# Query stage of a linear-attention and feed-forward kernel: the product with the key sums and the remainder of the tail weights on GpSimd, the tails stored in three transfers, the masked states made by PSUM bank

## The chip, the cores and the metric

The kernel runs on one core of one Trainium2 chip. The metric is the device time of one execution in microseconds (us). The unchanged kernel takes 1645.51 us, the median of three runs (1642.47 to 1647.66).

## The reference

Two networks are computed from independent inputs in float32. The first is a linear attention over 2048 rows of 576 columns with 32 heads of 18 columns: for queries and keys a learned 18x18 map per head and a double softmax (of the result and of its negative) give 36 features; the values are summed with the key features into a state per head, and the key features alone into key sums.

```
pq = einsum("bhsd,hdf->bhsf", q, w_phi); phi_q = concat(softmax(pq), softmax(-pq))    # the same for the keys
kv = einsum("bhsf,bhsd->bhfd", phi_k, v);  z = einsum("bhsf->bhf", phi_k)
num = einsum("bhqf,bhfd->bhqd", phi_q, kv)
den = einsum("bhqf,bhf->bhq", phi_q, z) + 1e-6
y = (num / den) @ wo
```

The second is a feed-forward network on rows of 576 columns with 4608 hidden columns: silu(x @ w_gate) * (x @ w_up), then @ w_down.

## The kernel before

Every float32 product on TensorE is made of parts: a value is split into a high part in TensorE's rounded format (a cast, mostly on ACT) and a remainder (a subtraction, mostly on DVE). A helper `split` does this, so many different instructions have its lines 58 and 59; `xw` issues products of the input with split weights, all under line 92.

The first 480 us hold the preparation, the key and value stage, and the **query stage**, from about 226 us. The key and value stage leaves the sums in three PSUM banks `kvp`, four, four and two blocks of up to 126 rows; one column more than the block is wide holds the key sums. At the boundary between the stages the key sums are copied out (`zc`), broadcast over 128 rows by matmuls with a 0/1 matrix (`ident`), and copied to `zb`; the states are multiplied with a mask that keeps the blocks of a head (`km`) and split into `KVH` and `KVL`.

The query stage takes 16 tiles of 128 rows, in pairs. For each tile `q_tile` does 28 matmuls with the folded query weights QH and QL into the one PSUM pair `p2`. This pair has no second buffer: the next tile's matmuls start when DVE's second subtraction `e<-p` has read the last of it. DVE and ACT make the softmax parts `e` (128x1152, both signs); `ez` is the product of `e` with `zb`, reduced over a head's columns to `y`; from it come the denominators, and `e` is scaled by them. `numer` then transposes `e` (`pt`), splits it (`ph`, `pl`), multiplies with the states (`po`) and splits the result (`oh`, `ol`); `project` multiplies with the split output weights `WOH` and `WOL`, and ACT copies the result (`so`) and stores it (`s_dram`). TensorE has other work to put between: gate and up products of five slices of the feed-forward network (`pe`), whose activation ACT and DVE finish (`h`) and whose weights ACT and DVE split (`wh`, `wl` from `raw`).

The stage also prepares eight **tails**, weight columns that the feed-forward network later reads back from device memory (`t_dram`). For each, SP loads 128x512 into the tile `tl` (two buffers), GpSimd forms three more blocks by four subtractions, ACT casts the 128x896 tile to `th` (one buffer), DVE subtracts `th` from `tl`, and GpSimd issues twelve stores of 32 rows: `th` twice and the remainder `tl` once, four each.

Within an engine instructions run in the order written. The order on each engine is set when the program is built: a scheduler places the instructions by dependence, by priority and by its own costs, and `tc.issue_after` bounds where the tails may go. A change of engine or of cost can thus move other instructions too. SP issues all loads of this stage and a share of the stores, ACT the stores of `so`.

Of the kernel before, what the change touches and what calls it, by code (L numbers as in the profile page):

```python
# [9 lines left out]
F32 = mybir.dt.float32  # L10
# [3 lines left out]
AX = mybir.AxisListType  # L14
PSUM = bass.MemoryType.PSUM

S, D, H, DH, F = 2048, 576, 32, 18, 4608
P = 128
# [7 lines left out]
GW = GH * DH  # L26
GROUPS = [(g * GW, min(GW, D - g * GW)) for g in range((D + GW - 1) // GW)]
NG = len(GROUPS)
# [9 lines left out]
def heads(ap):  # L38
    return ap.rearrange("p (h d) -> p h d", d=DH)


def spread(ap, n):
    return ap.unsqueeze(2).to_broadcast([P, n, DH])
# [3 lines left out]
def gated_hedgehog_kernel(ctx: ExitStack, tc, x, w_qk, w_v, w_phi, wo, w_gu, w_tail, w_down, ident_in, mask_in, out):  # L47
# [5 lines left out]
    nc = tc.nc  # L53
# [3 lines left out]
    def split(hi, lo, src):  # L57
        nc.scalar.copy(hi, src)  # L58
        nc.vector.tensor_sub(lo, src, hi)  # L59
# [15 lines left out]
    t_dram = dram.tile([TAILS, 4, 3, 32, 7, P], F32, name="t_dram")  # L75
# [3 lines left out]
    def block(t):  # L79
        return t // HT, (t % HT) // 4, slice((t % 4) * P, (t % 4 + 1) * P)  # L80

    def xw(ps, i, j, cols, wh, wl, stationary_x):
        pairs = []
        for k in range(2):
            b = XB[i][2 * j + k]
            for c in range(2):
                pairs += [(b[:, c, cols], w[:, k, c]) for w in (wh, wl)]
                pairs += [(b[:, 3 + c, cols], wh[:, k, c])]
            pairs += [(b[0:96, 2, cols], wh[0:96, k, 2])]
        for n, (a, b) in enumerate(pairs):  # L90
            l, r = (a, b) if stationary_x else (b, a)
            last = nc.tensor.matmul(ps, l, r, start=n == 0, stop=n == len(pairs) - 1)  # L92
        return last
# [32 lines left out]
    with ExitStack() as att:  # L126
        const = att.enter_context(tc.tile_pool(name="const", bufs=1))
        ident = const.tile([P, P], F32, name="ident")
# [3 lines left out]
        mask = const.tile([GW, GH, DH], F32, name="mask")  # L132
# [3 lines left out]
        with ExitStack() as wst:  # L136
# [4 lines left out]
            with ExitStack() as pst:  # L141
# [104 lines left out]
                for n in range(6):  # L246
                    k, c = divmod(n, 3)
                    src, vh = wv[n][:, 0:D], KVWH[:, k, c, D:2 * D]
# [18 lines left out]
            kps = kst.enter_context(tc.tile_pool(name="kps", bufs=1, space=PSUM, reuse_waits="tile"))  # L267
# [5 lines left out]
            def softmax_parts(ps, e):  # L273
                m = kk_pool.tile([P, 2, H], F32, name="m", bufs=1)
                p4 = ps[:, :, 0:HALF].rearrange("p a (h d) -> p a h d", d=DH)
                for s, op in enumerate((ALU.max, ALU.min)):
                    m3 = m[:, s].rearrange("p (a h) -> p a h", a=2)
                    nc.vector.tensor_reduce(m3, p4, axis=AX.X, op=op)
                    read.append(nc.vector.tensor_sub(e[:, s * D:(s + 1) * D].rearrange("p (a h d) -> p a h d", a=2, d=DH),
                                                     p4, m3.unsqueeze(3).to_broadcast([P, 2, H // 2, DH])))  # L280
                for s in range(2):
                    nc.scalar.activation(e[:, s * D:(s + 1) * D], e[:, s * D:(s + 1) * D], AF.Exp,
                                         scale=1.0 if s == 0 else -1.0)
                sm = kk_pool.tile([P, 2 * H], F32, name="sm")
                nc.vector.reduce_sum(sm, heads(e), axis=AX.X)
                nc.vector.reciprocal(sm, sm)
                return sm
# [137 lines left out]
            kvp = []  # L425
            pend = None
            order = [6, 7, 0, 1, 2, 3, 4, 5]
            for p in range(8):
# [29 lines left out]
                vx, vy, vw = (kps.tile([P, 512], F32, name=n) for n in ("vx", "vy", "vw"))  # L458
# [32 lines left out]
        with ExitStack():  # L491
            qc = att.enter_context(tc.tile_pool(name="qc", bufs=1, reuse_waits="tile"))
            KVH = qc.tile([GW, 2 * NG, GW], F32R, name="KVH")
            KVL = qc.tile([GW, 2 * NG, GW], F32R, name="KVL")
            zb = qc.tile([P, 2 * D], F32, name="zb")
            zc = qc.tile([GW, 2 * NG], F32, name="zc")
            for i in range(3):
                for j in range(4 if i < 2 else 2):
                    w = GROUPS[(4 * i + j) // 2][1]
                    nc.scalar.copy(zc[0:w, 4 * i + j:4 * i + j + 1], kvp[i][0:w, j, w:w + 1])  # L500
            for s in range(2):
                for a, m, name in ((0, 4, ("p2", "vw")[s]), (4, 1, ("vy", "vx")[s])):
                    o, w = GROUPS[a]
                    zp = kps.tile([P, 512], F32, name=name)
                    for g in range(a, a + m):
                        nc.tensor.matmul(zp[:, (g - a) * GW:(g - a) * GW + w],
                                         zc[0:w, 2 * g + s:2 * g + s + 1].to_broadcast([w, P]), ident[0:w, 0:w],
                                         start=True, stop=True)
                    nc.scalar.copy(zb[:, s * D + o:s * D + o + m * w], zp[:, 0:m * w])
            for i in range(2 * NG):  # L510
                o, w = GROUPS[i // 2]
                km = qc.tile([GW, GW], F32, name="km", bufs=2)
                nc.vector.tensor_mul(km[0:w, 0:w], kvp[i // 4][0:w, i % 4, 0:w],
                                     mask.rearrange("p h d -> p (h d)")[0:w, 0:w])
                split(KVH[0:w, i, 0:w], KVL[0:w, i, 0:w], km[0:w, 0:w])

        raw_x(order[7], 0, 1)
        raw_x(order[7], 2, 3)
# [4 lines left out]
        with ExitStack() as qst:  # L523
            qw = qst.enter_context(tc.tile_pool(name="qw", bufs=1, reuse_waits="tile"))
            qk = qst.enter_context(tc.tile_pool(name="qk", bufs=2, reuse_waits="tile"))
# [1 line left out]
            WOH = qw.tile([GW, NG, D], F32R, name="WOH")  # L527
            WOL = qw.tile([GW, NG, D], F32R, name="WOL")
            wrs = [qk.tile([P, 2, D], F32, name="oh", bufs=1), qk.tile([P, 2, D], F32, name="ol", bufs=1),
                   qk.tile([P, 2, D], F32, name="ez", bufs=1)]  # L530
            for g, (o, w) in enumerate(GROUPS):
                nc.sync.dma_start(wrs[g // 2][0:w, g % 2], wo[o:o + w, :])

# [8 lines left out]
            def tails(n):  # L542
                t = qk.tile([P, 7, P], F32, name="tl", bufs=2)
                hi = qk.tile([P, 7, P], F32R, name="th", bufs=1)
                nc.sync.dma_start(t[:, 0:4], w_tail[n])
                sub = nc.gpsimd.tensor_sub
                sub(t[:, 4], t[:, 2], t[:, 0])
                sub(t[:, 2], t[:, 3], t[:, 2])
                sub(t[:, 5], t[:, 3], t[:, 4])
                sub(t[:, 6], t[:, 1], t[:, 5])  # L550
                nc.scalar.copy(hi, t)
                nc.vector.tensor_sub(t, t, hi)
                for b, src in enumerate((hi.bitcast(F32), hi.bitcast(F32), t)):
                    for q in range(4):
                        nc.gpsimd.dma_start(t_dram[n, q, b], src[32 * q:32 * q + 32])

            last_e = []

            def q_tile(t):
                i0, j0, cols = block(t)  # L560
                pq = qps.tile([P, 2, 512], F32, name="p2")
                for i in range(2):
                    w = slice(i * HALF, (i + 1) * HALF)
                    xw(pq[:, i, 0:HALF], i0, j0, cols, QH[:, :, :, w], QL[:, :, :, w], True)
                e = qk.tile([P, 2 * D], F32, name="e", bufs=4)
                r = softmax_parts(pq, e)
                ez = qk.tile([P, 2 * D], F32, name="ez", bufs=1)
                nc.vector.tensor_mul(ez, e, zb)
                y = qk.tile([P, 2 * H], F32, name="y")
                nc.vector.reduce_sum(y, heads(ez), axis=AX.X)  # L570
                nc.vector.tensor_mul(y, y, r)
                den = qk.tile([P, H], F32, name="den")
                nc.vector.scalar_tensor_tensor(den, y[:, 0:H], DEN_EPS, y[:, H:], op0=ALU.add, op1=ALU.add)
                nc.vector.reciprocal(den, den)
                nc.vector.tensor_mul(r.rearrange("p (s h) -> p s h", s=2), r.rearrange("p (s h) -> p s h", s=2),
                                     den.unsqueeze(1).to_broadcast([P, 2, H]))
                last_e.append(nc.vector.tensor_mul(heads(e), heads(e), spread(r, 2 * H)))
                return e
# [55 lines left out]
            for n in range(TAILS):  # L634
                with tc.issue_after(last_e[3 * n // 2 + 2].ins):
                    tails(n)
# [82 lines left out]
    def stored(src, fill):  # L719
        h = h_tile()  # L720
        for r in range(2):
            nc.sync.dma_start(h[r], src[:, r * BT:(r + 1) * BT])
        for _ in range(2):
            fill()
        return h
# [280 lines left out]
    for i, n, f in units:  # L1006
# [3 lines left out]
        if f >= EARLY:  # L1010
            w = kept.pop() if i and kept else ready.pop(0)
# [4 lines left out]
        h = stored(h_dram[i, f], fill) if f < EARLY else gate_up(w, xo, fill, (i, f) == (0, EARLY))  # L1016
        if n % 2 == 0:
            g = {"f": (f, units[units.index((i, n, f)) + 1][2]), "h": [h]}
# [58 lines left out]
```

## Time and profile before

| | |
|---|---|
| median of three runs | 1645.51 us |
| profiled execution | 1645.38 us, its span 1643.6 us |
| TensorE matmul busy | 1606.3 us, 98% of the span |
| DVE busy | 1173.2 us, 71% |
| ACT busy | 723.1 us, 44% |
| GpSimd busy | 655.0 us, 40% |
| query stage | about 226 to 480 us |

Times in the profile run from the start of the span. The profiled execution is 1.8 us longer than its span and within 0.2 us of the median. PE is TensorE's matmul row, POOL is GpSimd, SPq and ACTq are the DMA queues that SP and ACT issue to. Matmuls overlap in the records, so the pace of a stretch is read from how many start in it.

### The profile page before, as it was taken

The page shows a single profiled execution, that of the slowest core. Times are in us where ns is not written, and L with a number is a line of the kernel's source. Part 1 is how long each engine was busy: PE and PEld are TensorE (multiplying, and loading weights), DVE is VectorE, ACT ScalarE, POOL GpSimd, SP SyncE. Part 2 cuts the span into 40 slices and gives each one's busy share as a digit, 9 for nine tenths or more (in the row PEclk, how much of TensorE's full clock was granted, in tenths as well). Part 3 has the DMA queues.
Part 4 walks back from the last instruction along what each step waited for, and adds up shares of the span by engine and source line. Part 5 has one row for each costly group of instructions (what it writes and reads, how often), then busy time and mean ns, then how long its engine had stood idle before and what let it go on. Part 6 is the DMA issues. An engine that isn't in the chain of part 4 may idle for free.

```text
span 1643.6 us, 25222 instructions
## 1 busy us (share of the span) xinstructions
PE 1606.3 (98%) x9385; PEld 1428.2 (87%) x9385; DVE 1173.2 (71%) x1733; ACT 723.1 (44%) x1407; POOL 655.0 (40%) x699
## 2 busy tenths in 40 slices
PE   6999999999999999999999999999999999999997
PEld 5899987999987788888888888888888888888886
DVE  7667768989862678788777788825566766666578
ACT  5533344454432554454444444445433433333334
POOL 3385661433213455355445365313243324133132
PEclk9999999999999999999999999999999999999999
DMA  9522243433239545555545554685454655555445
GB/s 293 197 79 78 88 133 114 119 109 110 79 108 329 183 162 172 182 171 177 174 167 181 178 176 156 222 299 157 134 159 138 199 183 172 168 180 182 139 114 173
DMA packets 121741, 268.47 MB, mean 163 GB/s; under 512 B 12786, under 2 KB 53362, under 8 KB 119826
## 3 DMA queue, kind: packets, MB, share of 16 engines
q1 hardware_dynamic: 106652, 246.49, 45.8%
q0 software_dynamic: 3072, 11.02, 2.5%
q10 hardware_dynamic: 11894, 9.35, 1.8%
q8 instruction: 74, 1.21, 0.3%
q14 instruction: 49, 0.40, 0.1%
HBM read 167.19 MB, written 99.61 MB: 162 GB/s over the span
## 4 chain that ended last, share of the span: by engine, by line
PE 66%; DVE 2%; DMA 1%; issue 1%; POOL 0%; ACT 0%; SPq 0%; DVEq 0%; ACTq 0%
PE pd L805 24%; PE px L706 24%; PE pw L706 12%; PE py L706 6%; PE pe L92 1%; DVE acc L777 0%; DVE w L59 0%; DMA rb<-in_B_w_down 0%; DMA ld<-in_B_w_gu 0%; DVE hh L59 0%; DMA X<-s_dram 0%; DVE dw L59 0%; DVE ha L766 0%; DVE acc L778 0%; DVE s L740 0%
## 5 line engine op out<-in xcount | busy, mean ns | idle before, releaser
L805 PEld LDWEIGHTS pd<-dw,hh 128*128 128x128 f32 x3048 | 433.6, 189 | 25.5 <-DVE dw L59 2.0
L805 PE MATMUL pd<-dw,hh 128*128 128x288 f32 x3048 | 449.7, 297 | 3.2 <-DVE dw L59 1.5
L706 PE MATMUL px<-X,w 128*128 128x512 f32 x1488 | 385.9, 393 | 2.1 <-ACT w L58 1.3
L706 PEld LDWEIGHTS px<-X,w 128*128 128x128 f32 x1488 | 270.2, 188 | 55.5 <-ACT s L735 4.0
L706 PE MATMUL pw<-X,w 128*128 128x512 f32 x744 | 191.8, 393 | 0.0
L706 PEld LDWEIGHTS pw<-X,w 128*128 128x128 f32 x744 | 139.1, 188 | 31.2 <-DVE s L740 0.3
L740 DVE TENSOR_TENSOR s<-pw,s 128x512 f32<-128x512 f32 x124 | 85.3, 688 | 103.2 <-ACT s L735 91.7
L930 DVE TENSOR_TENSOR acc<-pd,acc 128x576 f32<-128x576 f32 x128 | 96.3, 753 | 85.3 <-PE pd L805 85.1
L735 ACT COPY s<-px 128x512 f32<-128x512 f32 x124 | 72.6, 586 | 160.0 <-PE px L706 159.9
L92 PE MATMUL pe<-X,wh 128*128 128x512 f32 (+1 forms) x380 | 121.4, 401 | 5.3 <-ACT h L119 2.2
L58 ACT CAST hh<-ha 128x512 fp32r<-128x512 f32 x140 | 82.7, 619 | 92.9 <-PE pd L805 72.6
L59 DVE TENSOR_TENSOR hh<-ha,hh 128x512 fp32r<-128x512 f32 x140 | 109.9, 811 | 18.1 <-ACT hh L58 17.1
L902 POOL TENSOR_TENSOR hb<-hb 128x512 f32<-128x512 f32 x34 | 46.7, 1372 | 161.9 <-DVE hb L762 161.5
L59 DVE TENSOR_TENSOR w<-ld,w 128x512 fp32r<-128x512 f32 (+1 forms) x93 | 79.6, 858 | 37.6 <-ACT w L58 36.3
L706 PE MATMUL py<-X,w 128*128 128x512 f32 x372 | 97.7, 396 | 1.1 <-ACT py L747 1.1
L706 PE MATMUL px<-X,wt 96*128 96x512 f32 x248 | 97.9, 395 | 0.0
L915 POOL TENSOR_TENSOR ha<-ha 128x512 f32<-128x512 f32 x34 | 52.6, 1563 | 104.0 <-DVE hh L59 104.0
L889 POOL TENSOR_TENSOR h<-ha,hb 128x512 f32<-128x512 f32 x34 | 44.9, 1321 | 123.2 <-DVE ha L766 90.1
L58 ACT CAST w<-ld 128x512 fp32r<-128x512 f32 (+1 forms) x93 | 50.9, 549 | 90.1 <-POOL ld L696 58.0
L92 PEld LDWEIGHTS pe<-X,wh 128*128 128x128 f32 (+1 forms) x380 | 69.9, 189 | 20.6 <-DVE h L122 3.4
L693 POOL TENSOR_TENSOR ts<-ld 128x256 f32<-128x256 f32 x31 | 27.3, 880 | 140.7 <-issue 70.0
L747 ACT COPY py<-px 128x512 f32<-128x512 f32 x62 | 35.5, 572 | 103.7 <-PE px L706 84.4
(262 smaller groups left out, 3238.1 us busy)
## 6 DMA issues: line engine op xcount, KB each, us to landing
w_dram<-w SPq DMA_DIRECT2D x90, 512.0 KB, 2.9
w<-w_dram SPq DMA_DIRECT2D x90, 512.0 KB, 4.5
wt<-t_dram SPq DMA_DIRECT2D x61, 336.0 KB, 3.6
ld<-in_B_w_gu SPq DMA_DIRECT2D x31, 512.0 KB, 4.5
X<-sum_dram SPq DMA_DIRECT2D x8, 1280.0 KB, 11.4
rt<-in_B_w_down SPq DMA_DIRECT2D x33, 288.0 KB, 3.0
rb<-in_B_w_down SPq DMA_DIRECT2D x33, 288.0 KB, 4.3
w_dram<-w SPq DMA_DIRECT2D x30, 256.0 KB, 2.2
```

What stands on the lines that cost most here:

```text
L58: nc.scalar.copy(hi, src)
L59: nc.vector.tensor_sub(lo, src, hi)
L92: last = nc.tensor.matmul(ps, l, r, start=n == 0, stop=n == len(pairs) - 1)
L706: nc.tensor.matmul(ps, l, r, start=first and n == 0, stop=last and n == len(mm) - 1, skip_group_check=True)
L735: nc.scalar.copy(t, ps)
L740: nc.vector.tensor_add(t, ps, t)
L747: nc.scalar.copy(yp, xp)
L805: nc.tensor.matmul(ps, l, r, start=first and n == 0 and m == 0, stop=n == len(hs) - 1 and m == 2, skip_group_check=True)
L889: sub(s, g["h"][0][0], g["h"][0][1])
L902: nc.gpsimd.tensor_add(a21, a21, g["h"][1][1])
L915: sub(a12, a12, g["h"][0][0])
L930: nc.vector.tensor_add(a2, pd[:, :, 0:HALF], a2)
```

## The change

Four things change. First, key sums and masked states are made by bank: 3 copies of `zc` in place of 10, broadcasts into the `p2` pair and `vw` with 2 copies to `zb` in place of 4, and 3 masks, 3 casts and 3 remainders in place of 10 each. Second, the product `ez` goes from DVE (one 128x1152 instruction for a tile) to GpSimd (two of 128x576, each in a buffer of its own), and the reduction to `y` is cut in two as well. Third, the remainder of a tail goes from DVE to GpSimd. Fourth, a tail is stored by three transfers of 128 rows, two issued by ACT and one by SP, in place of twelve of 32 rows issued by GpSimd. Behind line 515 the lines of the program move up by one.

```
-            for i in range(3):
-                for j in range(4 if i < 2 else 2):
-                    w = GROUPS[(4 * i + j) // 2][1]
-                    nc.scalar.copy(zc[0:w, 4 * i + j:4 * i + j + 1], kvp[i][0:w, j, w:w + 1])
...
+            for i, n, w in banks:
+                nc.scalar.copy(zc[0:w, 4 * i:4 * i + n], kvp[i][0:w, 0:n, w])
+            zp, zq = kps.tile([P, 2, 512], F32, name="p2"), kps.tile([P, 512], F32, name="vw")
...
+            nc.scalar.copy(z2[:, :, 0:o], zp[:, :, 0:o])
+            nc.scalar.copy(z2[:, :, o:D], zq[:, 0:2 * (D - o)].rearrange("p (s n) -> p s n", s=2))
+            for i, n, w in banks:
+                km = qc.tile([GW, 4, GW], F32, name="km")
+                nc.vector.tensor_mul(km[0:w, 0:n, 0:w], kvp[i][0:w, 0:n, 0:w],
+                                     m4[0:w, 0:w].unsqueeze(1).to_broadcast([w, n, w]))
+                split(KVH[0:w, 4 * i:4 * i + n, 0:w], KVL[0:w, 4 * i:4 * i + n, 0:w], km[0:w, 0:n, 0:w])
...
-                   qk.tile([P, 2, D], F32, name="ez", bufs=1)]
+                   qk.tile([P, D], F32, name="ez", bufs=2).unsqueeze(1)]
...
                 nc.scalar.copy(hi, t)
-                nc.vector.tensor_sub(t, t, hi)
+                sub(t, t, hi)
                 for b, src in enumerate((hi.bitcast(F32), hi.bitcast(F32), t)):
-                    for q in range(4):
-                        nc.gpsimd.dma_start(t_dram[n, q, b], src[32 * q:32 * q + 32])
+                    (nc.scalar, nc.scalar, nc.sync)[b].dma_start(t_dram[n, :, b], src)
...
-                ez = qk.tile([P, 2 * D], F32, name="ez", bufs=1)
-                nc.vector.tensor_mul(ez, e, zb)
                 y = qk.tile([P, 2 * H], F32, name="y")
-                nc.vector.reduce_sum(y, heads(ez), axis=AX.X)
+                for s in range(2):
+                    ez = qk.tile([P, D], F32, name="ez", bufs=2)
+                    nc.gpsimd.tensor_mul(ez, e[:, s * D:(s + 1) * D], zb[:, s * D:(s + 1) * D])
+                    nc.vector.reduce_sum(y[:, s * H:(s + 1) * H], heads(ez), axis=AX.X)
```

`t_dram` is `[8, 4, 3, 32, 7, 128]`, so `t_dram[n, :, b]` is four separate blocks of 32 rows, and `t_dram[n, q, b]` was one such block.

GpSimd's order at the first tails, before. `slo` is the last of the key stage, the four `tl<-tl` rows are a tail's subtractions.

```order
137 L328 TENSOR_TENSOR slo<-sraw,shi 128x512
138 L547 TENSOR_TENSOR tl<-tl 128x128
139 L548 TENSOR_TENSOR tl<-tl 128x128
140 L549 TENSOR_TENSOR tl<-tl 128x128
141 L550 TENSOR_TENSOR tl<-tl 128x128
142 L547 TENSOR_TENSOR tl<-tl 128x128
143 L548 TENSOR_TENSOR tl<-tl 128x128
144 L549 TENSOR_TENSOR tl<-tl 128x128
145 L550 TENSOR_TENSOR tl<-tl 128x128
146 L555 DMA t_dram<-th 32x896 x8
147 L555 DMA t_dram<-tl 32x896 x4
```

Tails 0 and 1 follow each other, then the stores. GpSimd's order at the same place, after; the first two `ez` rows are the halves of tile 0, the third is the first half of tile 1:

```order
138 L568 TENSOR_TENSOR ez<-e,zb 128x576
139 L546 TENSOR_TENSOR tl<-tl 128x128
140 L547 TENSOR_TENSOR tl<-tl 128x128
141 L548 TENSOR_TENSOR tl<-tl 128x128
142 L549 TENSOR_TENSOR tl<-tl 128x128
143 L568 TENSOR_TENSOR ez<-e,zb 128x576
144 L546 TENSOR_TENSOR tl<-tl 128x128
145 L547 TENSOR_TENSOR tl<-tl 128x128
146 L548 TENSOR_TENSOR tl<-tl 128x128
147 L551 TENSOR_TENSOR tl<-tl,th 128x896
148 L549 TENSOR_TENSOR tl<-tl 128x128
149 L568 TENSOR_TENSOR ez<-e,zb 128x576
```

The four subtractions of tail 0 now stand between the two halves of tile 0's product, and tail 1's and the remainder of tail 0 ahead of tile 1's.

DVE's order where tile 1's maxima and subtractions are, before (`p_2521` is tile 1's pair):

```order
264 L286 RECIPROCAL sm<-sm 128x64
265 L278 TENSOR_REDUCE m<-p_2521 128x32
266 L279 TENSOR_TENSOR e<-p_2521,m 128x576
267 L278 TENSOR_REDUCE m<-p_2521 128x32
268 L279 TENSOR_TENSOR e<-p_2521,m 128x576
269 L59 TENSOR_TENSOR WOL<-oh,WOH 126x1152
```

And after (`p_2485` is tile 1's pair; both `y<-ez` are tile 0's):

```order
252 L285 TENSOR_REDUCE sm<-e 128x64
253 L569 TENSOR_REDUCE y<-ez 128x32
254 L286 RECIPROCAL sm<-sm 128x64
255 L278 TENSOR_REDUCE m<-p_2485 128x32
256 L569 TENSOR_REDUCE y<-ez 128x32
257 L279 TENSOR_TENSOR e<-p_2485,m 128x576
258 L570 TENSOR_TENSOR y<-y,sm 128x64
259 L278 TENSOR_REDUCE m<-p_2485 128x32
260 L63 TENSOR_TENSOR wl<-raw,wh 128x512
261 L64 TENSOR_TENSOR wh<-raw,wh 32x2x128
262 L572 SCALAR_TENSOR_TENSOR den<-y 128x32
263 L279 TENSOR_TENSOR e<-p_2485,m 128x576
```

Before, nothing but work on tile 1 stood between its maxima; now the second `y<-ez` of tile 0, which needs GpSimd's second half, stands ahead of both subtractions of tile 1.

ACT's order around the second tail's cast, before:

```order
234 L282 ACTIVATE e<-e 128x576
235 L618 COPY so<-p 128x288
236 L551 CAST th<-tl 128x896
237 L619 DMA s_dram<-so 128x288
238 L618 COPY so<-p 128x288
239 L619 DMA s_dram<-so 128x288
```

And after, around the fourth and fifth tails' casts:

```order
232 L550 CAST th<-tl 128x896
233 L58 CAST ph<-pt 72x512
234 L58 CAST oh<-po 126x256
235 L282 ACTIVATE e<-e 128x576
236 L553 DMA t_dram<-th 4x32x896
237 L58 CAST oh<-po 126x256
238 L553 DMA t_dram<-th 4x32x896
239 L282 ACTIVATE e<-e 128x576
240 L58 CAST oh<-po 72x256
241 L550 CAST th<-tl 128x896
242 L553 DMA t_dram<-th 4x32x896
243 L617 COPY so<-p 128x288
```

ACT now issues `th`'s stores itself, and the next tail's cast, which needs `th` free again, stands ahead of the copies `ph`, `oh` and `so` that TensorE waits for. All eight casts now stand between tile 0's and tile 6's softmax; before they were spread over the stage.

More of the change, by code (lines that the diff above doesn't have):

```diff
@@ L495, in gated_hedgehog_kernel @@
             zb = qc.tile([P, 2 * D], F32, name="zb")
-            zc = qc.tile([GW, 2 * NG], F32, name="zc")
-            for i in range(3):
-                for j in range(4 if i < 2 else 2):
-                    w = GROUPS[(4 * i + j) // 2][1]
-                    nc.scalar.copy(zc[0:w, 4 * i + j:4 * i + j + 1], kvp[i][0:w, j, w:w + 1])
[L501 to L515, printed above, removed]
+            zc = qc.tile([GW, 12], F32, name="zc")
+            m4 = mask.rearrange("p h d -> p (h d)")
+            banks = [(i, 4 if i < 2 else 2, GROUPS[2 * i][1]) for i in range(3)]
@@ new lines, in gated_hedgehog_kernel @@
+            for i, n, w in banks:
+                nc.scalar.copy(zc[0:w, 4 * i:4 * i + n], kvp[i][0:w, 0:n, w])
+            zp, zq = kps.tile([P, 2, 512], F32, name="p2"), kps.tile([P, 512], F32, name="vw")
+            for g, (o, w) in enumerate(GROUPS):
+                for s in range(2):
+                    d = zp[:, s, o:o + w] if g < NG - 1 else zq[:, s * w:s * w + w]
+                    nc.tensor.matmul(d, zc[0:w, 2 * g + s:2 * g + s + 1].to_broadcast([w, P]), ident[0:w, 0:w],
+                                     start=True, stop=True)
@@ new lines, in gated_hedgehog_kernel @@
+            z2, o = zb.rearrange("p (s n) -> p s n", s=2), GROUPS[-1][0]
+            nc.scalar.copy(z2[:, :, 0:o], zp[:, :, 0:o])
[5 more added lines that the diff above has]
+                split(KVH[0:w, 4 * i:4 * i + n, 0:w], KVL[0:w, 4 * i:4 * i + n, 0:w], km[0:w, 0:n, 0:w])
@@ L566, in q_tile @@
                 r = softmax_parts(pq, e)
-                ez = qk.tile([P, 2 * D], F32, name="ez", bufs=1)
-                nc.vector.tensor_mul(ez, e, zb)
                 y = qk.tile([P, 2 * H], F32, name="y")
-                nc.vector.reduce_sum(y, heads(ez), axis=AX.X)
+                for s in range(2):
+                    ez = qk.tile([P, D], F32, name="ez", bufs=2)
+                    nc.gpsimd.tensor_mul(ez, e[:, s * D:(s + 1) * D], zb[:, s * D:(s + 1) * D])
+                    nc.vector.reduce_sum(y[:, s * H:(s + 1) * H], heads(ez), axis=AX.X)
                 nc.vector.tensor_mul(y, y, r)
```

## The prediction

> **What bounds the kernel now.** The page first: its head and the busy times of the engines.
>
> ```profile
> span 1643.6 us, 25222 instructions
> PE 1606.3 (98%) x9385; PEld 1428.2 (87%) x9385; DVE 1173.2 (71%) x1733; ACT 723.1 (44%) x1407; POOL 655.0 (40%) x699
> ```
>
> The stage itself decides, so the windows come next (PE, PEld, DVE, ACT, POOL busy with their counts, granted clock, DMA share, GB/s).
>
> ```profile
> 250.00:260.00 10.00, 8.88 (x47) 7.10 (x45) 4.94 (x6) 8.08 (x10) 7.57 (x16) 1.00 0.61 198
> 260.00:270.00 10.00, 8.21 (x34) 6.33 (x34) 9.96 (x18) 3.62 (x5) 0.00 (x0) 1.00 0.17 57
> 300.00:400.00 100.00, 100.00 (x686) 91.90 (x685) 91.50 (x142) 45.30 (x80) 36.19 (x72) 1.00 0.37 109
> ```
>
> From 300 to 400 us TensorE has no idle time; DVE is 91% busy but nothing waits for it. Time saved on DVE or GpSimd there is worth nothing; time in which TensorE newly waits is lost in full, since nothing later is idle to take it back. The waits of PE between 225 and 500 us are the whole of what can be gained:
>
> ```profile
> PE pe L92 <- DVE h L122: 1.7, 1, 1.7
> PE p L614 <- ACT so L618: 1.3, 1, 1.3
> PE pt L588 <- DVE e L577: 1.3, 1, 1.3
> PE p L92 <- ACT zb L509: 1.1, 1, 1.1
> PE pe L92 <- ACT h L119: 0.9, 1, 0.9
> ```
>
> Together 6.3 us; all but the second (end of the stage) lie before 280 us: 5.0 us. A gain over 0.3%, 4.9 us and about what a measurement of this kernel tells from no change, would take nearly all of them.
>
> **The change part by part.** *States by bank.* The first query matmul waited 1.1 us for `zb`. Its new `p2` pair needs no copy any more, so it can start at 229.4 instead of 230.8; the fewer masks and casts run beside it. This removes the 1.1 us.
>
> *Work taken from DVE and GpSimd*, by the stage's groups of instructions (busy us, mean ns):
>
> ```profile
> L555 POOL DMA_DIRECT2D t_dram<-th x64 | 31.6, 501 | 42.7 <-ACT th L551 37.2 <-ACT oh L58 4.6 <-issue 0.2
> L568 DVE TENSOR_TENSOR ez<-e,zb 128x1152 f32<-128x1152 f32 x16 | 21.3, 1331 | 0.0
> L552 DVE TENSOR_TENSOR tl<-tl,th 128x896 f32<-128x896 f32 x8 | 8.6, 1080 | 0.0
> L551 ACT CAST th<-tl 128x896 fp32r<-128x896 f32 x8 | 7.5, 944 | 4.0 <-POOL tl L550 1.5 <-DVE tl L552 1.0 <-DVE den L574 0.8
> ```
>
> DVE loses 21.3 + 8.6 = 30 us and GpSimd some 47 us of issuing. By the windows these lie beside a full TensorE: worth 0. What GpSimd takes on is priced by its nearest rows:
>
> ```profile
> L889 POOL TENSOR_TENSOR h<-ha,hb 128x512 f32<-128x512 f32 x34 | 44.9, 1321 | 123.2 <-DVE ha L766 90.1
> L915 POOL TENSOR_TENSOR ha<-ha 128x512 f32<-128x512 f32 x34 | 52.6, 1563 | 104.0 <-DVE hh L59 104.0
> ```
>
> By width, half an `ez` costs 1.5 to 1.8 us (I take 1.5) and a tail's remainder 2.3 to 2.7 (2.5).
>
> *The first wait, tile 2.* The timeline around the first tail:
>
> ```profile
> 243.38 0.83 SPq L545 DMA_DIRECT2D tl<-in_B_w_tail  x2
> 250.03 0.46 POOL L547 TENSOR_TENSOR tl<-tl 128x128 f32<-128x128 f32 x1 [10.46 <-DMA h_dram<-h]
> 251.52 0.46 POOL L550 TENSOR_TENSOR tl<-tl 128x128 f32<-128x128 f32 x1
> 252.01 0.94 ACT L551 CAST th<-tl 128x896 fp32r<-128x896 f32 x1 [1.50 <-POOL tl L550]
> ```
>
> The load is issued at 243.4 behind those of the output weights, and the four subtractions end at 252.0; the change moves SP there by a few tenths only, so I take 251.6. Behind them now wait the second half of tile 0's `ez` (to 253.1), the `y` that DVE makes of it, and both subtractions of tile 1: y 0.7, e 0.8, y 0.2, m 0.75, wl 0.7, wh 0.45, den 0.2, e 0.8, ending at 257.7. Only then is `p2` free for tile 2, and nothing is ordered between. TensorE's pace:
>
> ```profile
> 231.00:234.00 3.00, 3.00 (x24) 3.00 (x24) 2.33 (x10) 1.19 (x6) 2.78 (x3) 1.00 0.00 0
> 261.81 0.39 PE L92 MATMUL pe<-X,wl 128*128 128x512 f32 x1
> 267.42 0.40 PE L92 MATMUL pe<-X,wl 128*128 128x512 f32 x1
> ```
>
> A query matmul takes 0.125 us; 24 `pe` start from the second row to before the third, 0.234 each. With 56 of each in front TensorE is there at 229.4 + 7.0 + 13.1 = 249.5. Wait: 8.2 us.
>
> *The stores.* How many DMA engines does a 4x32x896 store use? No transfer of before has an outermost count under 16, but ACT's queue and its issues, in the view of the transfers, show the rule for others (packets and MB; times x KB each; the last row is the 72-partition sibling, from the tile's own view):
>
> ```profile
> q10 hardware_dynamic: 11894, 9.35, 1.8%
> s_dram<-so ACTq DMA_DIRECT2D x32, 144.0 KB, 1.8
> y_dram<-acc ACTq DMA_DIRECT2D x8, 288.0 KB, 4.5
> x_dram<-xr ACTq DMA_DIRECT2D x8, 256.0 KB, 6.4
> ident<-in_ident ACTq DMA_DIRECT2D x1, 64.0 KB
> mask<-in_mask ACTq DMA_DIRECT2D x1, 62.0 KB
> phi_s<-in_A_w_phi ACTq DMA_DIRECT2D x1, 35.4 KB
> L228 ACTq DMA_DIRECT2D phi_s<-in_A_w_phi x1: 477/477/477, 2.3 to 2.3; - x1
> ```
>
> In pieces of 1152, 1152, 512, 512, 504, 72 and 72 bytes these are 32x128 + 8x256 + 8x512 + 128 + 126 + 504 + 72 = 11070 packets. The other 824 fit one closing packet for each engine used: 49 transfers of 128 partitions with 16 each (784), two of 126 with 14, one of 72 with 12. So the engines are the largest divisor, up to 16, of the outermost count. The new destination's is 4, its source's 128; an even division of both sides gives 4 engines. I take 4. The Trainium skill ("DMA: Bandwidth & Descriptors", section "Why a DMA increments its semaphore by 16 and not by 1") says that the largest count up to 16 that divides the slowest dimension of both patterns is used; by it, too, these stores have 4, and the 824 agree with it for equal sides.
>
> Their price:
>
> ```profile
> w_dram<-w SPq DMA_DIRECT2D x90, 512.0 KB, 2.9
> w_dram<-w SPq DMA_DIRECT2D x30, 256.0 KB, 2.2
> ```
>
> 256 KB more cost 0.7 us on 16 engines: 1.5 us fixed and 0.27 us for 100 KB. A store of 448 KB lands in 1.5 + 1.2 = 2.7 us on 16 engines, and takes 4.9 us of four engines' time, 6.4 with the fixed part. The 24 stores need 118 us on the same four engines; from the first cast to the eighth the order has 448 matmuls, 66 us at the pace of 300 to 400.
>
> Who waits: the next cast on ACT, and all behind it, waits until both `th` stores have landed (one buffer): 1.5 + 9.8 = 11.3 us, or 16.2 if SP's store of `tl` shares the engines. The load of tail n+2 waits until `tl`'s store n has landed; GpSimd's subtractions and the `ez` behind them wait for that load. Step by step:
>
> Tail 0's first `th` store is issued at 252.6, `tl`'s at 257.4 (after three subtractions and the remainder), the second `th` store behind ACT's exponentials at 258.9; the latter two land at about 268.5. Tail 1's cast, a table load and `h` end at 271.4; TensorE, at 268.0 through tile 2 and 28 `pe`, waits 3.4 us for a `pe` bank. The load of tail 2, 4.9 us,
>
> ```profile
> tl<-in_B_w_tail SPq DMA_DIRECT2D x8, 256.0 KB, 4.9
> ```
>
> lands at 273.4; four subtractions 1.9, remainder 2.5, `ez` 1.5, and 6.3 of DVE's rows lead to 285.6, when tile 3 may start; TensorE is there at 274.7 and waits 10.9. Then 91 matmuls at 0.146 us (100 us over 686) bring it to 298.9, where it needs an `oh` that ACT casts behind tail 3's cast. Tail 2's cast ends at 291.0, its `th` stores land between 302.4 and 307.3, the cast, `ph` and `oh` follow by 306.7 (middle): wait 7.8. The four later casts each make a loop of 0.95 plus 11.3 to 16.2, 14.7 in the middle, against the 58, 114, 25 and 44 matmuls that the order has between the waiting points: 8.5, 16.6, 3.7 and 6.4 us. Waits 6.2, 0, 11.0 and 8.3. After the eighth cast nothing of this is left.
>
> The sum: 8.2 + 3.4 + 10.9 + 7.8 + 25.5 = 55.8, less the 5.0 of old waits: +51 on the profiled execution's 1645.4 (its span and 1.8 around it; 0.1 from the median): **1696**. With all loops at 12.3 it is +41, with 17.2 and a dearer GpSimd +61; lower fixed times or less sharing could take off 8 more. This case alone: 1678 to 1712.
>
> One page speaks of a further cost: the Trainium skill ("TensorE: Matmul & The Clock Gate", section on the clock gate) has TensorE at half clock after an idle window of 3.4 us. By it the six waits of 6 us and more would add up to some 10 us, an estimate from that page; the trace grants 1.00 throughout the stage, and no wait there is over 1.7 us, so no run here shows it.
>
> **The rivals.** *Sixteen engines* (the source's 128 rows decide). For it: every 128-partition transfer above had 16. Against: the destination cannot be cut evenly into 16 blocks by its outermost count. Then a store lands in 2.7 us; the tile 2 wait stays at 8.2, tile 3's shrinks to 4.9 (load landing at 264.9 in place of 273.4, TensorE there at 271.3), the loops of 4.9 to 6 exceed only the 3.7, by about 1.2: 14.3 - 5.0 = +9, 1655, between 1645 and 1661.
>
> *Not slower.* The place is tile 0's second product half. It decides at 241.4: if tail 0's load lands then instead of 249.6, the half is done before TensorE needs `p2`, and with stores on 16 engines no wait is left: 1645.4 - 5.0 = 1640. Against: the load is issued at 243.4 before, and stands behind the output weights' loads in the new order as well.
>
> *GpSimd as the bound.* 32 halves and 8 remainders are 32 x 1.5 + 8 x 2.5 = 68 us for 47 taken off, over a stage of 250 us: 21 us more cannot bound it. If each half costs 1.8, the waits at tiles 2 and 3 grow by 0.3 each: no case of its own.
>
> **How the numbers follow.** Four engines 0.68, sixteen with the product half held 0.24, not held 0.08. Four engines is slower throughout. Of the 0.24 I count 0.15 slower (over 1650), 0.07 the same, 0.02 faster; of the 0.08, where a kept wait of a few us undoes the gain, 0.05 faster, 0.02 the same, 0.01 slower. Sums: faster 0.07, same 0.09, slower 0.84. The range 1650 to 1715 takes in 0.65 of the first case and the 0.15 of the second, 0.80; what it leaves out is the case without a loss below and the longest loops above.
>
> **What would show it.** Right: PE idle 8 us before tile 2's `p<-QH` around 250 to 258, released by DVE `e`, with DVE idle before `y` for GpSimd's `ez`; landing times of `t_dram` at 6 us and over; ACT idle before `th` for DMA `t_dram`; PE waits of 6 to 11 us behind ACT `oh` and `so` until about 367 us; none after. Wrong: `t_dram` landing in 3 us (the stores are wide), or casts that never wait for them, or no PE wait near 250 us.

## The result, and the profile after

The changed kernel takes 1741.36 us, the median of five runs (1739.99 to 1741.85); before it is 1644.71 in the same runs. The ratio is 1.0586, 95% interval 1.057 to 1.0601: slower by 97 us, where 51 were forecast and 1715 was the upper end of the range.

The page after, its head and busy times, TensorE's granted clock by slices and ACT's queue:

```profile
span 1738.2 us, 25121 instructions
PE 1629.0 (94%) x9385; PEld 1448.7 (83%) x9385; DVE 1155.5 (66%) x1711; ACT 719.9 (41%) x1389; POOL 669.0 (38%) x643
PEclk9999998777999999999999999999999999999999
q10 hardware_dynamic: 14006, 16.69, 3.0%
```

The span is 94.6 us longer. TensorE is busy 22.7 us longer (1629.0 against 1606.3) with the same 9385 matmuls, so it is idle 71.9 us longer. The slices with a clock of 7 and 8 tenths lie between 260 and 435 us, the stretch of the query stage in which TensorE now waits.

ACT's queue carried 14006 packets, 2112 more than before. The sixteen new stores of `th` have 128 rows each, 2048 packets. The 64 that are left are four closing packets for each store: four engines, as forecast. Windows of 20 us show it directly (DMA share last but one):

```profile
340.00:360.00 20.00, 5.26 (x21) 4.83 (x22) 2.70 (x4) 2.99 (x6) 5.86 (x7) 0.66 0.26 80
420.00:440.00 20.00, 19.99 (x145) 19.05 (x144) 14.16 (x23) 6.69 (x15) 2.86 (x2) 0.96 0.09 31
```

In the first, tail stores run with little else (one load of `tl` and two stores of `so` start in it): 0.26 of 16 engines is about four of them, and they move 80 GB/s. By that a store of 448 KB (459 thousand bytes) needs 5.7 us of the four, an estimate. The second window lies behind the last tail: TensorE is full again.

PE's waits from 225 to 500 us; before they came to 6.3 us:

```profile
PE p L613 <- ACT so L617: 34.2, 4, 11.9
PE p L613 <- ACT oh L58: 12.2, 2, 6.1
PE p L92 <- DVE e L279: 11.4, 2, 8.4
PE p L613 <- DVE ol L59: 7.1, 2, 6.8
PE pt L587 <- DVE pl L59: 5.8, 1, 5.8
PE pe L92 <- ACT h L119: 4.3, 1, 4.3
PE po L593 <- DVE ol L59: 2.5, 1, 2.5
PE pt L587 <- DVE e L576: 0.7, 1, 0.7
```

They are 78.2 us, 71.9 more than before: the whole idle difference. Behind them stand ACT's and SP's own waits for stores to land:

```profile
ACT th L550 <- DMA t_dram<-th: 56.1, 6, 15.0
ACT so L617 <- DMA s_dram<-so: 23.8, 2, 12.6
```

```profile
SPq L544 <- DMA t_dram<-tl: 74.9, 6, 14.3
```

The first row is the forecast loop: a cast of `th` that waits for the stores of the last. The second was not forecast: the store of `so` stands behind the stores of `th`. The third is SP: `tl` has two buffers, so a tail's load waits until the remainder of the tail before last has been stored. What stands behind that load is held too, on GpSimd the next tail's subtractions, and on DVE the `y` that needs the product behind them:

```profile
POOL tl L546 <- DMA tl<-in_B_w_tail: 73.7, 6, 17.4
DVE y L569 <- POOL ez L568: 67.7, 10, 21.3
```

The timeline shows the first five long waits of PE in order:

```profile
258.38 0.58 PE L92 MATMUL p<-QH,X 128*128 128x288 f32 x1 [8.41 <-DVE e L279]
276.09 0.80 PE L92 MATMUL pe<-X,wh 128*128 128x512 f32 x1 [4.30 <-ACT h L119]
285.06 0.58 PE L92 MATMUL p<-QH,X 128*128 128x288 f32 x1 [2.99 <-DVE e L279]
298.83 0.79 PE L593 MATMUL po<-ph,KVH 126*126 126x256 f32 x2 [2.53 <-DVE ol L59]
310.69 0.61 PE L613 MATMUL p<-WOH,oh 126*128 126x288 f32 x1 [6.13 <-ACT oh L58]
```

The wait before tile 2 is 8.41 us, ending at 258.4; 8.2 ending at 257.7 was forecast. The long waits behind these:

```profile
326.26 0.61 PE L613 MATMUL p<-WOH,ol 72*128 72x288 f32 x1 [6.76 <-DVE ol L59]
348.91 0.61 PE L613 MATMUL p<-WOH,oh 126*128 126x288 f32 x1 [10.63 <-ACT so L617]
358.70 1.07 PE L587 MATMUL pt<-ident,e 128*72 128x128 f32 x4 [5.83 <-DVE pl L59]
376.55 0.61 PE L613 MATMUL p<-WOH,oh 126*128 126x288 f32 x1 [6.04 <-ACT oh L58]
397.23 0.61 PE L613 MATMUL p<-WOH,oh 126*128 126x288 f32 x1 [11.90 <-ACT so L617]
415.73 0.61 PE L613 MATMUL p<-WOH,oh 126*128 126x288 f32 x1 [11.10 <-ACT so L617]
```

The first and the third of them end with DVE's `ol` and `pl`, which stood behind a `y` that waited for the held product. The second and the last end with a copy `so` that had itself waited 11.24 and 12.60 us for a store of `so` to land. The other two end behind a late cast of `th`, the eighth of which starts at 395.24; the last wait lies behind that cast.

### The profile page after: what moved, and what is told of

Read it like the earlier page. It is cut to its first block, busy times and chain, and to the rows that moved or that the text cites. A ratio compares the mean times of both kernels' runs of the same rounds, so it can differ in the third digit from the quotient of the medians.

```text
span 1738.2 us, 25121 instructions
## 1 busy us (share of the span) xinstructions
PE 1629.0 (94%) x9385; PEld 1448.7 (83%) x9385; DVE 1155.5 (66%) x1711; ACT 719.9 (41%) x1389; POOL 669.0 (38%) x643
## 3 DMA queue, kind: packets, MB, share of 16 engines
q10 hardware_dynamic: 14006, 16.69, 3.0%
## 4 chain that ended last, share of the span: by engine, by line
PE 82%; DMA 9%; DVE 4%; POOL 2%; ACT 1%; issue 1%; ACTq 0%; SPq 0%; POOLq 0%; DVEq 0%
PE px L705 22%; PE pd L804 22%; PE pw L705 11%; PE py L705 6%; PE p L92 5%; PE pe L92 4%; DMA t_dram<-tl 3%; DMA t_dram<-th 3%; PE p L613 2%; PE kvp L295 2%; PE vx L383 1%; PE po L593 1%; DMA s_dram<-so 1%; PE pt L587 1%; PE vw L383 1%
## 5 line engine op out<-in xcount | busy, mean ns | idle before, releaser
L613 PE MATMUL p<-WOH,oh 126*128 126x288 f32 (+1 forms) x160 | 53.5, 335 | 47.5 <-ACT so L617 35.3
L568 POOL TENSOR_TENSOR ez<-e,zb 128x576 f32<-128x576 f32 x32 | 45.9, 1441 | 123.5 <-ACT e L282 119.6
```

The costliest lines, as they stand in the source:

```text
L568: nc.gpsimd.tensor_mul(ez, e[:, s * D:(s + 1) * D], zb[:, s * D:(s + 1) * D])
L613: nc.tensor.matmul(ps[:, 0:HALF], a[0:w, g, jc], bw[0:w, g, n], start=k == 0, stop=k == 3 * NG - 1)
```

## The experiments

Theory A: the stores run on four engines, and the waits for their landing, with the clock that falls in them, are the loss. Its rivals are written with the runs. All runs but the first differ from the changed kernel in the order on the engines as well, so their totals are read with their traces.

**Wide stores, same order.**

```
-    t_dram = dram.tile([TAILS, 4, 3, 32, 7, P], F32, name="t_dram")
+    t_dram = dram.tile([TAILS, 3, 4, 32, 7, P], F32, name="t_dram")
-                    (nc.scalar, nc.scalar, nc.sync)[b].dma_start(t_dram[n, :, b], src)
+                    (nc.scalar, nc.scalar, nc.sync)[b].dma_start(t_dram[n, b].rearrange("q r m n -> (q r) m n"), src)
-        nc.sync.dma_start(wt.bitcast(F32), t_dram[n, q].rearrange("b r m n -> (b r) m n"))
+        nc.sync.dma_start(wt.bitcast(F32), t_dram[n, :, q])
```

> The changed kernel with the tails' blocks laid out in device memory as three times 128 rows, so that each of the 24 stores goes to 128 rows in one piece; every engine's order is the same as in the changed kernel. The 61 loads of the tails in the feed-forward stage then read three pieces of 32 rows each. Theory A (the stores ran on four DMA engines, and waits for their landing and the clock that fell in those waits are the loss): stores land in 3 us, the waits behind the casts go, the wait before tile 2 of about 8 us stays, the clock stays near 1.00 but for that wait; about 1655 us, if the loads, now on three engines, stay hidden (their DMA time is 6 to 7 us against 18 us between them). Theory B (what counts is that ACT and SP issue the stores and the single buffers make the casts wait, whatever the engines): 1715 to 1741 us. Theory C (GpSimd's product and remainder are the loss): 1715 to 1741 us.

Measured: 1669.98 us, ratio 1.0158 (1.0142 to 1.0174). Of 97 us 71 are gone with the layout alone. ACT's queue and ACT's wait for stores in this kernel:

```profile
q10 hardware_dynamic: 14198, 16.69, 2.8%
```

```profile
ACT th L550 <- DMA t_dram<-th: 1.9, 1, 1.9
```

192 packets more than 14006: sixteen stores with sixteen closing packets in place of four. The casts' wait falls from 56.1 to 1.9 us. Theories B and C fall as the main cause. The wait before tile 2 stays:

```profile
258.66 0.58 PE L92 MATMUL p<-QH,X 128*128 128x288 f32 x1 [8.65 <-DVE e L279]
```

Some 15 us more than forecast remain. TensorE is busy 8.4 us longer than before (1614.7 us), the slow clock that the forecast left out, and two waits are new: 4.9 us behind `ol`, 3.4 of them ending at 329 us, and 4.2 behind `h`, ending at 500 us near the stage's end. Before the wait for `h`, ACT waits 6.6 us for stores of `so`, while a load of a tail in three pieces, other loads and stores of `w` run; which of them is the cause was not tried.

**The stores alone, in the kernel before.**

```
-                    for q in range(4):
-                        nc.gpsimd.dma_start(t_dram[n, q, b], src[32 * q:32 * q + 32])
+                    (nc.scalar, nc.scalar, nc.sync)[b].dma_start(t_dram[n, :, b], src)
```

> The kernel before with the three four-block stores alone (two by ACT, one by SP); masks, product and remainder stay as before. Theory A: 24 stores at some 5 us of the same four engines, 120 us and more, in an order that spreads the casts further than the changed kernel's; 1680 to 1720 us. Theory C: 1645 us.

Measured: 1676.44 us, ratio 1.0191 (1.0177 to 1.0205), 4 us under the range but far from 1645: the stores alone cost 32 us where they are spread from 255.6 to 471.9 us. In the changed kernel's order, which has them from 251.8 to 398.4, the layout was worth 71. The same two waits of ACT are in this trace, 20.3 us of `th` for its stores and 17.0 of `so`.

**The states alone** (against the kernel before; the first hunk of the change and nothing else).

```
-            for i in range(2 * NG):
...
+            for i, n, w in banks:
+                km = qc.tile([GW, 4, GW], F32, name="km")
...
```

> The kernel before with the masked states and key sums by bank alone. All theories: the wait of 1.1 us for zb goes, nothing else; 1643 to 1645 us.

Measured: 1642.21 us, ratio 0.9988 (0.9979 to 0.9996). The wait for `zb` is not in its trace. It is 1.9 us faster (0.7 to 3.5 by the interval), more than the 1.1 expected and 0.8 under the range given; 1.1 is not told from 1.9 by these runs.

**The product alone** (against the kernel before).

```
-                nc.vector.tensor_mul(ez, e, zb)
...
+                for s in range(2):
+                    ez = qk.tile([P, D], F32, name="ez", bufs=2)
+                    nc.gpsimd.tensor_mul(ez, e[:, s * D:(s + 1) * D], zb[:, s * D:(s + 1) * D])
+                    nc.vector.reduce_sum(y[:, s * H:(s + 1) * H], heads(ez), axis=AX.X)
```

> The kernel before with the product ez on GpSimd alone, in halves. Theories A and B: the tail's subtractions stand between the halves here too, one wait of about 8 us before tile 2, and the waits of before mostly gone; 1645 to 1655 us. Theory C: over 1690 us.

Measured: 1653.43 us, ratio 1.0054 (1.0038 to 1.0069), as theory A has it. Its trace also shows what one wait does to TensorE's clock. Windows of 2 us (PE busy and count, granted clock, DMA share, GB/s):

```profile
252.00:254.00 2.00, 1.13 (x5) 1.00 0.94 371
254.00:256.00 2.00, 0.00 (x0) 1.00 0.11 43
256.00:258.00 2.00, 0.00 (x0) 0.80 0.00 0
258.00:260.00 2.00, 0.10 (x1) 0.50 0.79 194
260.00:262.00 2.00, 2.00 (x9) 0.50 0.93 238
262.00:264.00 2.00, 2.00 (x10) 0.50 0.39 110
264.00:266.00 2.00, 2.00 (x15) 0.99 0.54 115
```

The wait is 6.77 us, from 253.1 to 259.9. Some 4 us into it the granted clock falls to 0.50, and it comes back some 4 us after the work does. In those 4 us the work of 2 is done, so a wait of 6.8 us costs about 9, an estimate from these windows.

**Stores cut in two.** Theory D is that four engines are a matter of size, not of the outermost count.

```
-                    (nc.scalar, nc.scalar, nc.sync)[b].dma_start(t_dram[n, :, b], src)
+                    for q in range(0, 4, 2):
+                        (nc.scalar, nc.scalar, nc.sync)[b].dma_start(t_dram[n, q:q + 2, b], src[32 * q:32 * q + 64])
```

> The changed kernel with every tail store cut in two, of two blocks of 32 rows each: twice as many transfers of half the size. Theory A (the engines of a transfer are the largest divisor up to 16 of the outermost counts): each runs on two engines, the same ones; while only stores run the share of the DMA engines in use is 2 of 16, and the bytes, 11 MB, need twice the time of four engines: some 110 to 135 us more than the changed kernel, 1850 to 1890 us. Theory D (four is a property of the size or of the whole transfer's rows, 64 rows being enough for 16 engines): smaller stores land sooner, under 1741 us.

Measured: 1800.92 us in one run: slower by 60, so D falls, but by half of what A said. The number of engines is as the rule has it:

```profile
320.00:340.00 20.00, 11.11 (x63) 10.59 (x64) 8.94 (x15) 2.96 (x6) 3.62 (x2) 0.76 0.13 45
q10 hardware_dynamic: 14006, 16.69, 2.8%
```

0.13 is two engines of 16, and 32 stores of `th` with two closing packets each are again 64. The size was missed because the order moved: the stores now run from 251.5 to 503.0 us by their first and last issue, against 251.8 to 398.4, and TensorE works between them. The engines' time doubled; what it costs depends on what the order puts beside it.

**All stores on SP.**

```
-                    (nc.scalar, nc.scalar, nc.sync)[b].dma_start(t_dram[n, :, b], src)
+                    (nc.sync, nc.sync, nc.sync)[b].dma_start(t_dram[n, :, b], src)
```

> The changed kernel with all three stores of a tail issued by SP, so that ACT's queue holds only the stores of so. Theory E (the 24 us that ACT waited for stores of so came from standing behind th's stores in ACT's own queue): so's waits vanish, 1700 to 1720 us. Theory F (the four engines are shared by all queues, so a store of so waits on any of them): so's stores still wait several us, 1730 us and over. In both the four-engine stores bound the tails.

Measured: 1733.03 us, ratio 1.0547 (1.053 to 1.0563).

```profile
ACT th L550 <- DMA t_dram<-th: 55.9, 5, 15.9
ACT so L617 <- DMA s_dram<-so: 4.2, 2, 2.4
```

The wait of `so` falls from 23.8 to 4.2 us, as theory E has it: most of it came from standing behind `th`'s stores in ACT's own queue, as far as a run with another order on the engines can show. The total falls by 8 only, where E said 21 and more, and 1733 is what F said. The casts' wait for stores is as long as it was.

**The wide stores with the product back on DVE** (against the wide stores above).

```
-                    nc.gpsimd.tensor_mul(ez, e[:, s * D:(s + 1) * D], zb[:, s * D:(s + 1) * D])
...
+                nc.vector.tensor_mul(ez, e, zb)
+                y = qk.tile([P, 2 * H], F32, name="y")
+                nc.vector.reduce_sum(y, heads(ez), axis=AX.X)
```

> The kernel of the first run of the first batch (tails in pieces of 128 rows) with the product ez back on DVE in one instruction. Theory A with the tile 2 wait priced by the held product: the wait of 8.7 us and about 2 us of slow clock after it go; 1657 to 1661 us. If the held product is not what that wait is for: 1668 to 1672.

Measured: 1660.21 us, ratio 1.0093 (1.0068 to 1.0117), 10 us less than with the product on GpSimd. No wait for tile 2 is in its trace, so the held product has a share of its own in the loss. Some 16 us over the kernel before are left, of which 5.2 are longer matmuls; the remainder on GpSimd, the stores issued by ACT and SP and the loads of three pieces were not tried apart.

**The stores put back** (product and remainder stay on GpSimd).

```
-                    (nc.scalar, nc.scalar, nc.sync)[b].dma_start(t_dram[n, :, b], src)
+                    for q in range(4):
+                        nc.gpsimd.dma_start(t_dram[n, q, b], src[32 * q:32 * q + 32])
```

> The changed kernel with the stores alone put back: twelve transfers of 32 rows issued by GpSimd. Theory A: the tile 2 wait of 8 us with its slow clock stays, no cast waits long for a store; 1652 to 1664 us. Theory C (GpSimd's remainder and product are the loss): over 1700 us.

Measured: 1659.00 us, ratio 1.0089 (1.0071 to 1.0107). As forecast; with the stores alone put back 82 of the 97 us are gone. The largest wait left is before tile 2, and the second behind the scaling of `e`:

```profile
PE p L92 <- DVE e L279: 10.7, 2, 10.4
PE pt L588 <- DVE e L577: 5.9, 5, 2.7
```

**Two stores in place of three**, on four engines as before.

```
-                for b, src in enumerate((hi.bitcast(F32), hi.bitcast(F32), t)):
-                    (nc.scalar, nc.scalar, nc.sync)[b].dma_start(t_dram[n, :, b], src)
+                for b, src in enumerate((hi.bitcast(F32), t)):
+                    (nc.scalar, nc.sync)[b].dma_start(t_dram[n, :, b], src)
...
-        nc.sync.dma_start(wt.bitcast(F32), t_dram[n, q].rearrange("b r m n -> (b r) m n"))
+        nc.sync.dma_start(wt[0:32].bitcast(F32), t_dram[n, q, 0])
+        nc.sync.dma_start(wt[32:96].bitcast(F32), t_dram[n, q].rearrange("b r m n -> (b r) m n"))
```

> The changed kernel with two stores for a tail in place of three: th is stored once, and the feed-forward stage reads its rows twice, by two loads for each piece (32 and 64 rows) in place of one. The stores stay on four DMA engines. Theory A with loops set by the bytes of all stores of a tail (5.7 us of the four engines for each, by the 80 GB/s of a stretch with stores alone): a loop from cast to cast shrinks from about 19.7 to 14 us, seven loops by about 40; 1695 to 1715 us. Theory G (loops set by fixed latencies and by the order of issue): 1730 us and over.

Measured: 1709.15 us, ratio 1.0406 (1.0378 to 1.0435), as theory A with bytes has it; G falls. The last casts of `th` in this kernel's timeline, and then those of the changed kernel:

```profile
328.71 0.94 ACT L550 CAST th<-tl 128x896 fp32r<-128x896 f32 x1 [9.71 <-POOL tl L549]
342.10 0.94 ACT L550 CAST th<-tl 128x896 fp32r<-128x896 f32 x1 [8.88 <-POOL tl L549]
355.62 0.94 ACT L550 CAST th<-tl 128x896 fp32r<-128x896 f32 x1 [7.83 <-POOL tl L549]
```

```profile
308.95 0.94 ACT L550 CAST th<-tl 128x896 fp32r<-128x896 f32 x1 [8.00 <-DMA t_dram<-th]
328.49 0.94 ACT L550 CAST th<-tl 128x896 fp32r<-128x896 f32 x1 [10.37 <-DMA t_dram<-th]
349.85 0.93 ACT L550 CAST th<-tl 128x896 fp32r<-128x896 f32 x1
374.58 0.94 ACT L550 CAST th<-tl 128x896 fp32r<-128x896 f32 x1 [7.72 <-DMA t_dram<-th]
395.24 0.94 ACT L550 CAST th<-tl 128x896 fp32r<-128x896 f32 x1 [15.01 <-DMA t_dram<-th]
```

With two stores these loops are 13.4 and 13.5 us; with three 19.5, 21.4, 24.7 and 20.7. Two and three times 5.7 us, with the fixed 1.5 and the cast, would be 13.9 and 19.6. The earlier loops are less even, so the whole is a better measure: from the first cast to the eighth the two kernels take 105.6 us (250.07 to 355.62) and 144.4 (250.85 to 395.24), 39 less where 40 were expected. What the casts wait for is another thing, though: with two stores it is mostly GpSimd's subtractions, which wait for a load that waits for the remainder's store. That the bytes on the four engines set this path too is argued from the sizes, not shown.

**A faster version**: the states by bank, and each tail one query tile later.

```
-                with tc.issue_after(last_e[3 * n // 2 + 2].ins):
+                with tc.issue_after(last_e[3 * n // 2 + 3].ins):
```

> A version meant to be faster: the kernel before with the masked states and key sums by bank, and every tail allowed one query tile later, so that ACT's first casts of th do not stand in front of h. All theories: the wait for zb (1.1 us) is gone, and of the waits for h before 262 us (2.6 us) some may go; 1639 to 1643 us, not to be told from the states alone if the order only shifts.

Measured: 1640.28 us, ratio 0.9976 (0.9963 to 0.9989): the fastest of all here, but not told from the states alone by these intervals. The two waits for `h` were not removed (1.7 and 1.4 us in its trace, 1.7 and 0.9 before).

## Why the prediction was right in kind and half in size

The kind of loss was foreseen: stores on four engines, casts that wait for them, and a product held on GpSimd. The size was not: the path through the later loops was priced too short, it was said to end with the eighth cast, and the clock was left out.

*Four engines* were right: 64 closing packets, a DMA share of 0.26, and 71 us back when the layout alone is changed.

*Tile 2's wait* was right, 8.41 for 8.2 us. Its prices were near: half an `ez` took 1.44 us for 1.5, the remainder 2.09 for 2.5.

*Up to tail 3's cast* 30.3 us of waits were forecast; the five rows of the timeline give 24.4. Tile 3 was released at 285.1, for 285.6 forecast, but waited 2.99 us and not 10.9: TensorE reached it late itself, through the wait for `h` before it and a clock of 0.73 from 270 to 280 us.

*The later loops* are the first term that was mis-sized: 25.5 us forecast, 78.2 - 24.4 = 53.8 measured. The loop was put at 14.7 us, the middle between two and three stores at 4.9 us each; the four loops took 19.5 to 24.7. All three stores of a tail share the four engines, at some 5.7 us each, which makes 19.6. With 19.6 the same four loops give 11.1, 3.0, 15.9 and 13.2, together 43.2. The trace has 42.0 up to the wait that ends at 397.2. The sums agree better than the parts, which is partly luck: in the third loop, the longest, ACT issues the second `th` store only at 363.8, behind a cast `ph` that had waited 9.96 us for TensorE.

*"After the eighth cast nothing of this is left"* is the step that failed outright. A wait of 11.1 us, ending at 415.7, is left there: the store of `so` stands behind the eighth tail's stores on ACT's queue.

*What releases the waits* was seen in part. The forecast has TensorE wait for copies behind a cast. Of the 53.8 us such waits are 17.9 (6.04 and 11.90). Those behind a store of `so`, which the forecast does not have, are 21.7 (10.63 and 11.10). Those behind a product held by a tail's load, which it has for tile 3 only, are 12.6 (6.76 and 5.83). Three waits under 1 us are the rest. How much each path would cost without the others was not tried.

*The clock* is the second term, and the sum left it at zero: 22.7 us of longer matmuls. The windows of the product's run show the mechanism. The changed kernel has nine waits over 4 us, so each goes with about 2.5 us. The Trainium skill ("TensorE: Matmul & The Clock Gate", its Part 1 on the clock gate) has the clock at half after an idle window of 3.4 us; by it the prediction's estimate was some 10 us for the waits forecast. The trace agrees with the rule: the granted clock fell to 0.50 about 4 us into the wait of 6.77 us. The trace of before could not have refuted it in this stage, since no wait there was over 1.7 us.

*The old waits*: 5.0 us were to go; the account takes off all 6.3 of before. It is 24.4 + 53.8 + 22.7 - 6.3 = 94.6, the difference of the spans; the forecast was 30.3 + 25.5 + 0 - 5.0 = 50.8. Its case by itself was put at 1678 to 1712; the dearest sum that it works out is +61, or 1706.

*Sixteen engines* was priced at 1655 as a rival; the run made so gives 1670. There too the clock, 8.4 us, was missing, and with it the waits behind `ol` and behind `h`, 4.9 and 4.2 us.

## What to carry to other kernels

Count the engines of a transfer from the outermost dimension of both sides before merging transfers: here four blocks of 32 rows in one transfer had four engines, two blocks two, and a layout in which the 128 rows lie together sixteen. Then price a loop with all the bytes that go through its engines, and every wait of TensorE over some 4 us with about 2 us more for the clock. Follow each in-order queue to its end: a store that itself has all the engines (`so`) still waited behind those that had four. Work moved off DVE, for which nothing waited here, gained nothing, while the queue that it was put on became a wait for what stood behind it (9 to 10 us for the product).

## What the runs showed of the hardware that was not expected

Transfers on the same few engines, from one queue or two, delay each other's landing far more than their own time: a `th` store issued at 258.3 let the next cast start only at 272.6, 14 us later, for some 5.7 us of its own transfer time. The tail's other two stores were issued before it, at 251.8 by ACT and at 255.6 by SP. And a store of 144 KB (`so`), 1.8 us to landing before, held ACT for up to 12.6 us behind two such stores.
